# Attention and an FFT-mixed FFN on one core: batch 0's scores and values as two streams, index tables behind the first loads, and new durations in the planner

## The chip, the cores and the metric

The kernel runs on one core of one Trainium2 chip. The metric is the device time of one execution in microseconds (us). Five engines each work through an instruction queue of their own, in order: PE (matrix products), DVE, ACT and POOL (element work), and SP, which here only issues DMA transfers. Semaphores tie the queues together.

## The reference

q, k and v have 8 batches, 12 heads, 448 rows and 64 columns. All arithmetic of the reference is float32.

```python
scores = q @ k.transpose(0, 1, 3, 2) / sqrt(64)
attn   = maximum(scores, 0) ** 2 / 448
x      = (attn @ v) with the heads side by side     # (8, 448, 768)
u      = x + real(fft(fft(x, axis=1), axis=2))
un     = (u - mean(u)) / sqrt(var(u) + 1e-6)        # over the 768 columns
out    = u + maximum(un @ w_ch1, 0) @ w_ch2         # 768 -> 3072 -> 768
```

## The kernel before

**Stages.** Matrix products take bf16 operands. For each batch the heads are worked in pairs (m, 0 to 5). q and k are turned on PE for batches 0 and 1 (`turn_on_pe`, L505, copied out of PSUM at L510), later by DMA transposes (L469 copies, L481 transposes). A pair has four score chunks (c, 0 to 3). For each chunk there are two score products (L736), a Relu on ACT out of PSUM (`squares`, L761) and a square, mostly on DVE (`square`, L776, on ACT at L773). Four finished chunks feed eight value products (L718), which add up in one PSUM bank. `fold` then takes that bank out to bf16 in two halves (`leave`, L542 for batch 0, L557 or L554 later) and adds and subtracts its mirrored halves (L587, L589). The sums go through a DFT over the channels (`first_channels`, L1187, for batch 0; `mix`, L1212, later) and one over the rows (`rows` in `first_tail`, L823 and L827; `mix_rows`, L1026 and L1030, later), which gives u. Rows of u are normalised (un), turned (L926 for the first group of rows, L994 for the second), and go through the FFN: first layer L1452 with its Relu on DVE (L1424) or ACT (L1426), second layer L1477, L1503 and L1583, added to u at L1438.

**Tables.** `build_dft` makes cosine and sine tables. POOL writes index rows (`dft_indices`, L245 to L251), DVE turns them into phases (`turns`, L304 to L306), and ACT takes the sine (L310). The row tables (seqm, nseq) need two sets of 240 columns, the channel tables (chan, three of them) one set of 386 columns each. The pairs 3 to 5 need the channel table's second half with its sign changed, `chan_neg`, made by DVE (L333).

**The order of the work.** The body runs under a manual schedule. Each part is a generator that asks for an engine with `need(engine, duration, what must be ready, buffers)`; `Streams.run` keeps a planned clock for each engine and always emits the instruction that can start first by that clock (ties by rank). The durations (`mm`, `act`, `dve`, `dve2`, `SWITCH`, `LATENCY`) and the planned landing of loads thus decide the order in each queue, and nothing else. The emitted order is fixed; on the chip each queue waits at its own semaphores.

**Batch 0.** `attention(0)` is one stream: it emits the scores of one chunk at a time, and the eight value products of a pair together, after the scores of the same step. Where PE has nothing planned, `warming` emits filler products on zeros (L1661) until the DFT over the channels of batch 0 is done. `attentions` runs batches 1 to 7, interleaved with the FFN of earlier rows; `LEAD` limits how far it runs ahead.

**The first tail.** After batch 0's row DFT (four sets of rows, t from 0 to 3) `first_tail` is written out by hand: statistics on DVE (`stats` L847, `aggregate` L853), root on ACT (L859), `scale` on DVE (L867, L868), `norm` on POOL (L900) for the first three sets and on ACT (L902) and DVE (L905) for the last, `copy` of u (L876), `turn` on PE (L926, with filler products L924 and L931), `unload` out of PSUM (L941). The FFN starts when all four are unloaded.

**Loads.** POOL issues them in the order of `loading`: batch 0's three groups of q, k, v (L376), q and k of batch 1, the first weight in twelve pieces (L406), v of batch 1 among the second weight in four pieces (L416). SP issues the DMA transposes, the stores of u and the output.

Of the kernel before, what the change touches and what calls it, by code (L numbers as in the profile page):

```python
# [57 lines left out]


LATENCY = {"PE": 0.28, "ACT": 0.18, "DVE": 0.16, "POOL": 0.2, "SP": 0.1}  # L60


class Streams:
# [29 lines left out]
    def run(self):  # L93
        end = {}
        while self.streams:
# [61 lines left out]
def dve2(n):  # L157
    return Port(n / 1920 + 0.14)


SWITCH = 0.13


@with_exitstack
def kernel(
# [132 lines left out]
    def build_dft():  # L298
# [27 lines left out]
        for m in range(3):  # L326
            e = yield need("DVE", 1.5, [indices_ready])
            y = early_hid if m == 2 else work.tile([128, 4 * KH], FP32, name="dfty", tag=("u1A", "u1B")[m], bufs=1)
            turns(y[:, 2 * KH:4 * KH], y[:, 0:2 * KH], col2, row[:, 4 + m:5 + m], 2 * KH, m % 2)
            yield from sine(chan[m][:, 0, :], y[:, 0:2 * KH], 2 * KH, e, -1, halfpi)  # L330
            yield from sine(chan[m][:, 1, :], y[:, 2 * KH:4 * KH], 2 * KH, e)
            e = yield need("DVE", 0.3, [dft_ready])
            nc.vector.tensor_scalar(chan_neg[:, m], chan[m][:, :, KH:], -1.0, None, op0=ALU.mult)  # L333
            dft_ready.t = chan_ready[m].t = e + LATENCY["DVE"]

# [26 lines left out]
    def load_group(i, which=(0, 1, 2)):  # L362
# [3 lines left out]
        for x, (nm, src) in enumerate((("q", q), ("k", k), ("v", v))):  # L366
            if x not in which:
                continue
            if b == 0 and x < 2:
                e = yield need("POOL", 0.85)  # L370
                t = first_qk[x][:R, g]
            else:
                e = yield need("POOL", 0.85, bufs=[BQ[x] if x == 2 else BQ[x][home(i)]])
                t = work.tile([R, HG, 4 * Dh], BF16, name=f"{nm}n",
                              tag="vn" if x == 2 else f"{nm}n{home(i)}", bufs=3 if x == 2 else 1)
            nc.gpsimd.dma_start(out=t, in_=src[b, hs].rearrange("h (p j) d -> p h (j d)", j=4))  # L376
            loads[i][x] = t.rearrange("p h (j d) -> p j h d", j=4)
# [12 lines left out]
            if i == NG + 1 and x == 1:  # L390
                yield need("POOL", 3.6)
                mirrors()
# [28 lines left out]
    def loading():  # L421
# [101 lines left out]
    def fold(b, m, F, av, give, av_end):  # L523
# [4 lines left out]
        def leave():  # L528
# [4 lines left out]
            else:  # L533
# [125 lines left out]
    def attention(b, left=None):  # L659
# [9 lines left out]
        while pa < NB:  # L669
# [38 lines left out]
            for part in ("scores", "values") if few else ("values", "scores"):  # L708
# [19 lines left out]
                for i in range(p, p + n):  # L728
                    m, c = divmod(i, 4)
                    qT, kT, flat = turned[b][m // 2]  # L730
                    wide = R if b < 2 else 128
                    k0 = (2 * c + m % 2) * R
                    sc = BS.take()
                    for h in range(2):
                        ps = slice(h * Dh, (h + 1) * Dh)
                        nc.tensor.matmul(sc[:wide, h, 0:S].rearrange("k (c q) -> k c q", c=4),  # L736
                                         lhsT=flat[ps, k0:k0 + wide], rhs=qT[ps, m % 2],
                                         start=True, stop=True)
# [4 lines left out]
                    if b == 0 and i == NB - 1:  # L743
                        first_scores.t = e
            p += n
# [4 lines left out]
            if av_end is not None:  # L750
                left = None
                yield from fold(bv, mv, Fv, av, give, av_end)

    def squares(b, scs, sqs):
        for i, sc, t in scs:
            e = yield need("ACT", act(2 * S) - 0.03, [t + LATENCY["PE"]], [BSQ])
            at = min(sq_ids)
# [41 lines left out]
    def first_tail(pcs):  # L799
# [88 lines left out]
        def norm(t, hf, en):  # L888
# [3 lines left out]
            if en == "POOL":  # L892
                deps.append(u_done[ch][i])
            d = {"ACT": act(D // 2), "DVE": dve(D // 2), "POOL": 2.0}[en]
            e = yield need(en, d, deps, [BUN[ch]] if i == 0 and hf == 0 else [])
# [11 lines left out]
            t_un[t][hf] = e + LATENCY[en]  # L907
            if min(t_un[t]) or en == "POOL":
                half_un[ch][i].t = max(t_un[t])
# [24 lines left out]

        def unload(t, en):
            n, idn, c0, w = turned_cols(t)
            g = groups[0][2]
            src = pts[t][0][:, :, 0:384].rearrange("p h (m w) -> p h m w", w=128)[:, :, :, 0:w]
            dst = g[:, :, c0:c0 + w].rearrange("p (h m) w -> p h m w", h=2)
            last = yield need(en, (act if en == "ACT" else dve)(6 * w), [done[t][0]])  # L940
            (nc.scalar.copy if en == "ACT" else nc.vector.tensor_copy)(dst, src)  # L941
            BS.give(pts[t][0], last)
            first_un[t].t = last + LATENCY["ACT"]
# [6 lines left out]
        for t in range(3):  # L950
# [35 lines left out]

    second_un = [Cell() for _ in range(5)]

# [394 lines left out]
    def ffn(b):  # L1383
# [83 lines left out]
        for c in WHOLES[b]:  # L1467
# [3 lines left out]
            for hf in range(2):  # L1471
# [192 lines left out]

    LEAD, MIXED, SPARE, ELASTIC = 2.6, 1, 0.5, (1, 99)
    with tc.manual_schedule():
# [7 lines left out]
        sch.add(mixes(), (1, 1))  # L1674
        sch.add(attention(0), (0, 0))
        for i in range(2):
# [40 lines left out]
```

## Time and profile before

| | |
|---|---|
| median of 3 runs | 584.73 us (584.64 to 585.35) |
| the profiled execution | 584.67 us, its span 582.8 us |
| mean granted PE clock | 0.997 |
| PE filler products L1661 | 204, from 1.3 to 39.4 us |
| first row product of batch 0 (L823) | 40.64 us |
| first FFN product (L1452) | 53.63 us |
| last FFN product (L1583) | starts at 578.97 us |

Times in the profile are us from the first instruction. In the lists of instructions the columns are start, length, engine, line, operation, tiles written and read, shapes and count; what stands in brackets is how long the engine was idle before it and who released it. A row of several merged instructions has the length from the first one's start to the last one's end. Consecutive instructions of one engine overlap a little, so start to start is the better price. In a table of windows each engine has its busy time and its instructions (x).

### The profile page before, as it was taken

The page shows a single profiled execution, that of the slowest core. Times are in us where ns is not written, and L with a number is a line of the kernel's source. Part 1 is how long each engine was busy: PE and PEld are TensorE (multiplying, and loading weights), DVE is VectorE, ACT ScalarE, POOL GpSimd, SP SyncE. Part 2 cuts the span into 40 slices and gives each one's busy share as a digit, 9 for nine tenths or more (in the row PEclk, how much of TensorE's full clock was granted, in tenths as well). Part 3 has the DMA queues.
Part 4 walks back from the last instruction along what each step waited for, and adds up shares of the span by engine and source line. Part 5 has one row for each costly group of instructions (what it writes and reads, how often), then busy time and mean ns, then how long its engine had stood idle before and what let it go on. Part 6 is the DMA issues. An engine that isn't in the chain of part 4 may idle for free.

```text
span 582.8 us, 11457 instructions
## 1 busy us (share of the span) xinstructions
PE 572.9 (98%) x4476; PEld 365.7 (63%) x4476; DVE 406.4 (70%) x927; ACT 335.0 (57%) x511; POOL 133.7 (23%) x188
## 2 busy tenths in 40 slices
PE   8999999999999999999999999999999999999997
PEld 7566556544455546556857667568577786868684
DVE  5978667986669988787787878987946852222222
ACT  5866873587745787676668748777654340304040
POOL 8534021411115313421333032303300230000000
PEclk9998999999999999999999999999999999999999
DMA  9999999776947997699579987993433353031201
GB/s 120 206 211 227 222 210 134 173 131 95 181 57 189 207 172 168 116 216 167 122 123 207 180 153 147 200 176 115 126 75 100 118 151 99 30 94 36 79 30 55
DMA packets 133493, 81.85 MB, mean 140 GB/s; under 512 B 77504, under 2 KB 128704, under 8 KB 133440
## 3 DMA queue, kind: packets, MB, share of 16 engines
q0 software_dynamic: 40320, 33.63, 38.2%
q1 hardware_dynamic: 93120, 47.50, 36.3%
q8 instruction: 35, 0.57, 0.4%
q14 instruction: 18, 0.15, 0.1%
HBM read 62.91 MB, written 26.25 MB: 153 GB/s over the span
## 4 chain that ended last, share of the span: by engine, by line
PE 88%; DVE 6%; ACT 4%; issue 1%; POOL 0%; DVEq 0%; ACTq 0%; POOLq 0%
PE psF L1452 37%; PE psF L1583 26%; PE psS L736 6%; PE psF L718 5%; PE psF L1503 3%; PE psF L1477 3%; PE psS L1212 2%; ACT sq L761 2%; DVE sq L776 2%; PE psS L718 1%; PE psS L823 1%; PE psS L1026 1%; PE psS L1187 1%; PE psF L505 0%; ACT un L1087 0%
## 5 line engine op out<-in xcount | busy, mean ns | idle before, releaser
L1452 PE MATMUL psF<-unT,w 128*128 128x256 bf16 (+2 forms) x1728 | 229.8, 291 | 1.2 <-ACT unT L999 0.9
L1452 PEld LDWEIGHTS <-w 128*128 128x128 bf16 x1728 | 165.9, 98 | 61.6 <-issue 11.5
L761 ACT ACTIVATE sq<-psS 112x896 bf16<-112x896 f32 x192 | 164.4, 918 | 38.4 <-PE psS L736 38.0
L1426 ACT ACTIVATE hT<-psF 128x512 bf16<-128x512 f32 (+3 forms) x169 | 87.9, 532 | 116.6 <-PE psF L1452 115.8
L776 DVE TENSOR_TENSOR sq<-sq 112x896 bf16<-112x896 bf16 x161 | 100.6, 638 | 16.6 <-ACT sq L761 15.6
L1583 PEld LDWEIGHTS <-hT 128*128 128x128 bf16 x792 | 76.0, 98 | 54.4 <-issue 5.8
L1438 DVE TENSOR_TENSOR o<-psF,o 128x384 f32<-128x384 f32 x92 | 50.9, 553 | 44.8 <-PE psF L1583 39.6
L1583 PE MATMUL psF<-w,hT 128*128 128x384 bf16 x462 | 81.7, 326 | 0.3 <-DVE hT L1424 0.2
L736 PE MATMUL psS<-qkT 64*128 64x448 bf16 (+1 forms) x384 | 51.6, 359 | 1.2 <-ACT qkT L510 0.4
L718 PE MATMUL psF<-sq,vn 112*64 112x448 bf16 x320 | 37.9, 358 | 0.3 <-DVE o L1438 0.3
L557 DVE TENSOR_SCALAR xT<-psF 128x224 bf16<-128x224 f32 x58 | 19.8, 383 | 26.3 <-PE psF L718 26.2
L376 POOL DMA_DIRECT2D vn<-in_v_dram x24 | 17.3, 720 | 76.0 <-PE psS L736 67.7
L1059 POOL TENSOR_TENSOR u<-tp,xn 112x385 f32<-112x385 f32 (+2 forms) x14 | 13.3, 953 | 93.1 <-DVE tp L1041 81.5
L1583 PE MATMUL psF<-wsum,hT 128*128 128x384 bf16 x198 | 34.6, 326 | 0.0
L736 PEld LDWEIGHTS <-qkT 64*128 64x128 bf16 (+1 forms) x384 | 15.9, 102 | 28.7 <-issue 21.2
L376 POOL DMA_DIRECT2D qn<-in_q_dram x21 | 15.5, 739 | 69.9 <-DVE qkr L469 49.6
L718 PEld LDWEIGHTS <-vn 112*64 112x64 bf16 x384 | 17.8, 109 | 21.4 <-issue 13.7
L773 ACT ACTIVATE sq<-sq 112x896 bf16<-112x896 bf16 x31 | 29.5, 956 | 0.5
L1068 DVE BATCH_NORM_STATS2 stats<-u 112x6 f32<-112x384 f32 (+2 forms) x56 | 28.4, 541 | 0.0
L1087 ACT ACTIVATE un<-u,nmr,rstd 112x768 bf16<-112x768 f32 (+2 forms) x22 | 22.4, 1025 | 7.3 <-DVE nmr L1074 5.0
L1477 PE MATMUL psF<-w,hT 128*128 128x384 bf16 x144 | 25.1, 326 | 0.0
L1503 PE MATMUL psF<-w,hT 128*128 128x384 bf16 x144 | 24.7, 326 | 0.0
(166 smaller groups left out, 612.6 us busy)
## 6 DMA issues: line engine op xcount, KB each, us to landing
out_dram<-o SPq DMA_DIRECT2D x56, 192.0 KB, 2.2
vn<-in_v_dram POOLq DMA_DIRECT2D x24, 224.0 KB, 5.9
qn<-in_q_dram POOLq DMA_DIRECT2D x21, 224.0 KB, 5.3
kn<-in_k_dram POOLq DMA_DIRECT2D x21, 224.0 KB, 5.5
w<-in_moe_w_ch_dram POOLq DMA_DIRECT2D x12, 384.0 KB, 14.5
w<-in_moe_w_ch_dram POOLq DMA_DIRECT2D x4, 1152.0 KB, 20.5
utop<-u SPq DMA_DIRECT2D x12, 336.0 KB, 3.1
o<-utop SPq DMA_DIRECT2D x16, 192.0 KB, 3.8
```

The source lines that it names most:

```text
L376: nc.gpsimd.dma_start(out=t, in_=src[b, hs].rearrange("h (p j) d -> p h (j d)", j=4))
L718: nc.tensor.matmul(av[h * Dh:(h + 1) * Dh, 0:S], lhsT=vn[:, c, h0 + h, :], rhs=sq[:, h, :], start=(c == 0), stop=(c == 3))
L736: nc.tensor.matmul(sc[:wide, h, 0:S].rearrange("k (c q) -> k c q", c=4), lhsT=flat[ps, k0:k0 + wide], rhs=qT[ps, m % 2], start=True, stop= ...
L761: nc.scalar.activation(r, sc[:R, :, 0:S], AF.Relu)
L773: nc.scalar.activation(r, r, AF.Square)
L776: nc.vector.tensor_tensor(r, r, r, op=ALU.mult)
L1426: nc.scalar.activation(hs, ps, AF.Relu)
L1438: nc.vector.tensor_tensor(o, pc[:, 0:DH], o, op=ALU.add)
L1452: nc.tensor.matmul(ph[:, i * N:(i + 1) * N], lhsT=w1_sb[m][hf][:, (jj + i) * 128:(jj + i + 1) * 128], rhs=unT[:, m, 0:N], start=(m == 0), ...
L1477: nc.tensor.matmul(pc[:, 0:DH], lhsT=block(j, c), rhs=w2(j, hf), start=(j == 0), stop=(j == JC - 1))
L1503: nc.tensor.matmul(pc[:, 0:DH], lhsT=block(2 * i + k, c), rhs=weights[i], start=(start and i == 0), stop=(i == KP - 1), skip_group_check=True)
L1583: nc.tensor.matmul(pc[:, 0:DH], lhsT=lhs[i], rhs=rhs[i], start=(start and i == 0), stop=(i == KP - 1), skip_group_check=True)
```

## The change

- **Two streams for batch 0.** `first_attention` emits score chunks only; for each pair it adds a stream `first_values`, which asks for the two value products of each chunk as soon as that chunk is squared, instead of all eight together.
- **The planner's durations.** `mm`, `act` and `SWITCH` are shorter; an engine's planned clock advances by less than the duration on ACT and DVE (`OVERLAP`); loads of batches 2 and later are planned to land earlier (2.0 and 1.0 instead of 14.0 and 7.0 us of allowance); `LEAD` is 2.8 instead of 2.6. This changes the order on all engines through the whole program.
- **Tables.** The index rows come right after the first q and k loads, ahead of the identity matrix and the first v load. `chan_neg` is made on POOL (`negative`).
- **The last exit of batch 0.** For pair 5 one half of the exit is on ACT, the other on DVE.
- **First tail.** Statistics and aggregate of the last set come ahead of the third set's norm; the last unload is split, one half on ACT and one on DVE, and goes ahead of the last copies of u.
- **Weights.** Three of the four loads of the second weight wait in POOL's queue behind the third norm (`first_norms`). `w2_free` is set by the last whole block alone.

```diff
+OVERLAP = {"ACT": 0.12, "DVE": 0.07}
-            self.engine[eng] = start + dur
+            self.engine[eng] = start + max(dur - OVERLAP.get(eng, 0.0), 0.5 * dur)
 def mm(n):
-    return n / 2400 + 0.006
+    return n / 2400 + 0.002
 def act(n):
-    return n / 1200 + 0.2
+    return n / 1200 + 0.17
-SWITCH = 0.13
+SWITCH = 0.1
...
-            e = yield need("DVE", 0.3, [dft_ready])
-            nc.vector.tensor_scalar(chan_neg[:, m], chan[m][:, :, KH:], -1.0, None, op0=ALU.mult)
-            dft_ready.t = chan_ready[m].t = e + LATENCY["DVE"]
+            sch.add(negative(m, dft_ready.t), (0, 0))
+
+    def negative(m, t):
+        e = yield need("POOL", 0.4, [t])
+        nc.gpsimd.tensor_scalar(chan_neg[:, m], chan[m][:, :, KH:], -1.0, None, op0=ALU.mult)
+        dft_ready.t = chan_ready[m].t = e + LATENCY["POOL"]
...
-            ready[i][x].t = sch.dma(e, GRP, 360e3, "sw") + (1.5 if g else 0.0, 3.0, 14.0, 7.0)[min(b, 3)]
+            ready[i][x].t = sch.dma(e, GRP, 360e3, "sw") + (1.5 if g else 0.0, 3.0, 2.0, 1.0)[min(b, 3)]
             if i == 0 and x == 1:
-                yield need("POOL", 0.7)
-                make_identity(nc, ident)
-            if i == 0 and x == 2:
                 e = yield need("POOL", 1.1)
                 dft_indices()
                 indices_ready.t = e + LATENCY["POOL"]
+                yield need("POOL", 0.7)
+                make_identity(nc, ident)
...
         yield from load_group(NG + 2, (2,))
+        yield need("POOL", 0.0, [first_norms])
         yield from load_w2([1, 2, 3])
...
-            if b == 0:
+            if b == 0 and m == MC - 1:
+                t1 = yield need("ACT", act(HS), [av_end], [BX[m]])
+                nc.scalar.activation(xa[0], xa[1], AF.Copy, scale=1.0 / (64.0 * S))
+                t = yield need("DVE", dve(HS), [av_end])
+                nc.vector.tensor_scalar(xb[0], xb[1], 1.0 / (64.0 * S), None, op0=ALU.mult)
+                t = yield need("DVE", 2 * dve2(NS), [t1 + LATENCY["ACT"]])
+            elif b == 0:
...
+    def first_attention():
+        F, sqs = [], {}
+        for i in range(4 * MC):
+            m, c = divmod(i, 4)
+            e = yield need("PE", mm(S) + 2 * SWITCH, [turned_at[0][m // 2][m % 2]], [BS])
+            sc = score(0, i)
+            if i == 4 * MC - 1:
+                first_scores.t = e
+            sqs[i] = [None, Cell(), None]
+            sch.add(squares(0, [(i, sc, e - SWITCH)], sqs), (0.2, 0.2))
+            if c == 3:
+                if m % 2 == 1:
+                    BQT.free.append(e)
+                sch.add(first_values(m, F, sqs), (0.1, 0.1))
+
+    def first_values(m, F, sqs):
+        vn, h0 = loads[m // 2][2], 2 * m % HG
+        for c0, c1 in ((0,1),(1,2),(2,3),(3,4)):
+            e = yield need("PE", (c1 - c0) * mm(S) + 2 * SWITCH,
+                           [sqs[4 * m + c][1] for c in range(c0, c1)] + [ready[m // 2][2]],
+                           [BF] if c0 == 0 else [])
+            if c0 == 0:
+                av = BF.take()
+            for c in range(c0, c1):
+                sq, _, at = sqs.pop(4 * m + c)
+                sq_ids.append((e, at))
+                BSQ.free.append(e)
+                for h in range(2):
+                    nc.tensor.matmul(av[h * Dh:(h + 1) * Dh, 0:S], lhsT=vn[:, c, h0 + h, :], rhs=sq[:, h, :],
+                                     start=(c == 0), stop=(c == 3))
+        if m % 2 == 1:
+            BQ[2].free.append(e)
+        yield from fold(0, m, F, av, lambda when: BF.give(av, when), e - SWITCH + LATENCY["PE"])
...
-        def unload(t, en):
+        def unload(t, en, part=None):
...
+            hs = slice(0, 2) if part is None else slice(part, part + 1)
+            src = pts[t][0][:, hs, 0:384].rearrange("p h (m w) -> p h m w", w=128)[:, :, :, 0:w]
+            dst = g[:, :, c0:c0 + w].rearrange("p (h m) w -> p h m w", h=2)[:, hs]
...
         yield from stats(3, 0)
+        yield from stats(3, 1)
+        yield from aggregate(3)
         yield from scale(2)
         yield from norm(2, 0, "POOL")
-        yield from stats(3, 1)
-        yield from aggregate(3)
         yield from turn(0, 0)
         yield from root(3)
...
         yield from unload(2, "ACT")
+        yield from turn(3, 0)
+        yield from unload(3, "ACT", 0)
+        yield from unload(3, "DVE", 1)
         yield from copy(3, 0, "ACT")
-        yield from turn(3, 0)
-        yield from unload(3, "DVE")
         yield from copy(3, 1, "DVE")
...
-            w2_free.t = e + LATENCY["PE"]
+            if c == WHOLES[b][-1]:
+                w2_free.t = e + LATENCY["PE"]
...
-    LEAD, MIXED, SPARE, ELASTIC = 2.6, 1, 0.5, (1, 99)
+    LEAD, MIXED, SPARE, ELASTIC = 2.8, 1, 0.5, (1, 99)
...
-        sch.add(attention(0), (0, 0))
+        sch.add(first_attention(), (0, 0))
```

More of the change, by code (lines that the diff above doesn't have):

```diff
@@ L729, in attention @@
                     m, c = divmod(i, 4)
[L730 to L738, printed above, removed]
+                    sc = score(b, i)
                     scs.append((i, sc, e - SWITCH - (4 * mm(S) + SWITCH if values and few else 0.0)
@@ L752, in attention, with score @@
                 yield from fold(bv, mv, Fv, av, give, av_end)
+    def first_attention():
[15 more added lines that the diff above has]
+        for c0, c1 in ((0,1),(1,2),(2,3),(3,4)):
+            e = yield need("PE", (c1 - c0) * mm(S) + 2 * SWITCH, [sqs[4 * m + c][1] for c in range(c0, c1)] + [ready[m // 2][2]],
+                           [BF] if c0 == 0 else [])
[11 more added lines that the diff above has]
+        yield from fold(0, m, F, av, lambda when: BF.give(av, when), e - SWITCH + LATENCY["PE"])
+    def score(b, i):
+        m, c = divmod(i, 4)
+        qT, kT, flat = turned[b][m // 2]
+        wide = R if b < 2 else 128
+        k0 = (2 * c + m % 2) * R
+        sc = BS.take()
+        for h in range(2):
+            ps = slice(h * Dh, (h + 1) * Dh)
+            nc.tensor.matmul(sc[:wide, h, 0:S].rearrange("k (c q) -> k c q", c=4), lhsT=flat[ps, k0:k0 + wide],
+                             rhs=qT[ps, m % 2], start=True, stop=True)
+        return sc
     def squares(b, scs, sqs):
         for i, sc, t in scs:
-            e = yield need("ACT", act(2 * S) - 0.03, [t + LATENCY["PE"]], [BSQ])
+            e = yield need("ACT", act(2 * S), [t + LATENCY["PE"]], [BSQ])
             at = min(sq_ids)
@@ L893, in norm @@
                 deps.append(u_done[ch][i])
-            d = {"ACT": act(D // 2), "DVE": dve(D // 2), "POOL": 2.0}[en]
+            d = {"ACT": act(D // 2), "DVE": dve(D // 2), "POOL": 1.0}[en]
             e = yield need(en, d, deps, [BUN[ch]] if i == 0 and hf == 0 else [])
@@ L933, in turn @@
                 yield need("PE", 16 * 0.055)
-        def unload(t, en):
+        def unload(t, en, part=None):
             n, idn, c0, w = turned_cols(t)
             g = groups[0][2]
-            src = pts[t][0][:, :, 0:384].rearrange("p h (m w) -> p h m w", w=128)[:, :, :, 0:w]
-            dst = g[:, :, c0:c0 + w].rearrange("p (h m) w -> p h m w", h=2)
-            last = yield need(en, (act if en == "ACT" else dve)(6 * w), [done[t][0]])
+            hs = slice(0, 2) if part is None else slice(part, part + 1)
+            src = pts[t][0][:, hs, 0:384].rearrange("p h (m w) -> p h m w", w=128)[:, :, :, 0:w]
+            dst = g[:, :, c0:c0 + w].rearrange("p (h m) w -> p h m w", h=2)[:, hs]
+            last = yield need(en, (act if en == "ACT" else dve)((6 if part is None else 3) * w), [done[t][0]])
             (nc.scalar.copy if en == "ACT" else nc.vector.tensor_copy)(dst, src)
+            t_un[t][part or 0] = last
+            if part == 0:
+                return
+            if part == 1:
+                last = max(t_un[t])
             BS.give(pts[t][0], last)
@@ L984, in first_tail @@
         sch.add(turn_rows(uns[0][1], max(t_un[1]), 128, rev[:, 63:127], 0, 64, "DVE", second_un[0]), (1, 1))
-    second_un = [Cell() for _ in range(5)]
+    second_un, first_norms = [Cell() for _ in range(5)], Cell()
     def turn_rows(un, t, n, idn, c0, w, en, done):
```

4 lines of the change are left out of this document (2 added, 2 removed).

## The prediction

> **What bounds the kernel now.** I read the page first (busy shares, slices), then the DVE timeline of the opening, the windows by stage, the waits, and the ACT timeline around 120 us.
>
> ```profile
> PE 572.9 (98%) x4476; PEld 365.7 (63%) x4476; DVE 406.4 (70%) x927; ACT 335.0 (57%) x511; POOL 133.7 (23%) x188
> ```
>
> PE looks full, but 204 of its matmuls are fillers (L1661) that do no work, all before 39.4 us. The windows show the stages:
>
> ```profile
> core 0: us, PE busy (x) PEld busy (x) DVE busy (x) ACT busy (x) POOL busy (x), PEclk, DMA share, GB/s
> 7.93:39.52 31.59, 30.42 (x385) 19.32 (x385) 28.43 (x66) 26.30 (x35) 15.29 (x46) 1.00 1.18 197
> 40.64:52.74 12.10, 10.75 (x112) 7.96 (x112) 8.90 (x26) 7.96 (x18) 9.05 (x11) 1.00 1.24 222
> 60.00:460.00 400.00, 397.82 (x2920) 238.11 (x2917) 317.18 (x718) 261.63 (x398) 96.92 (x110) 1.00 0.85 152
> ```
>
> From 60 us on PE stands still for only 2.2 us of 400, so the end moves only by what the opening (batch 0's attention, 7.93 to 39.52), the first tail (40.64 to 52.74) and the few PE gaps later give. In the opening the busiest worker that does real work is DVE, 28.43 of 31.59 us, with its waits in view:
>
> ```profile
> 7.93 0.62 DVE L510 COPY qkT<-psF 128x896 bf16<-128x896 bf16 x1 [0.32 <-PE psF L505]
> ...
> 11.18 0.63 DVE L776 TENSOR_TENSOR sq<-sq 112x896 bf16<-112x896 bf16 x1 [0.18 <-ACT sq L761]
> ...
> 13.81 0.27 DVE L333 TENSOR_SCALAR channeg<-chan 128x386 bf16<-128x386 bf16 x1 [0.38 <-ACT chan L310]
> ...
> 38.26 0.69 DVE L542 TENSOR_SCALAR xT<-psF 128x224 bf16<-128x224 f32 x2 [0.96 <-PE psF L718]
> ```
>
> DVE waits for ACT while four squares are ready one by one, then for the sine, and at the end 0.96 us for the last values, which stood on PE behind 16 transposes and 14 matmuls of L1187.
>
> **The sum is made** against the profiled execution: 584.67 us, its span 582.8 and 1.87 around it. The median of the runs is 584.73, so I add the change to the median. About 0.2%, 1.2 us, is what a measurement of this kernel can tell from no change.
>
> **Opening, DVE's work.** Both kernels start at the same DVE copy (7.93): it waits for the first loads, whose issues do not move. By starts (overlaps of consecutive instructions taken off):
> - One set of table steps L304, L305, L306 moves ahead of that copy: 13.99 to 15.57 is 1.58 us. It fits there: the index iotas now follow the k load (its issue ends at 2.96) instead of the v load (4.21), 1.25 earlier, so the first tables end at 7.62 - 1.25 = 6.37 and the set at 7.95.
> - The three sign copies L333 go to POOL: 13.81 to 13.99, 3 x 0.18 = 0.54.
> - One half of the last exit L542 goes to ACT: 0.30 (17.70 to 18.00).
>
> Together 2.42 us less. **DVE's waits**, by starts: before, 0.31 for the first square, 0.27 for each of three more (0.80 apart, while a square takes 0.53 back to back: 2.67 for five), 0.47 for L333, 0.7 for four later squares, 1.04 for the last exit: 3.3. After: ACT now does both sines of table 0 and the copy L510 ahead of the squares. Sines start at 6.40; three at 0.59, two at 0.51, the copy 0.80: first square at 10.0, done at 10.9; DVE is free at about 10.05, so 0.85; then 0.27, and 0.78 where a sine (0.51) stands between. From there on ACT needs 24 x 0.80 + 4 x 0.51, done by 31.3 and always ahead of DVE. At the end three quarters of the last values are already on PE, since each quarter follows its square; what is left is 0.5. Sum 2.4, so 0.9 less. Opening: -3.3.
>
> The halved exit is not parallel: in the built program the DVE half carries a wait for the ACT half, which the change writes first. So 0.36 and 0.30 in a row stand in place of 0.68; nothing is gained there beyond DVE's 0.30. The same with the last unload of the tail.
>
> **What the POOL copies cost.** A POOL tensor operation on 768 columns takes 0.98 (L900), so 386 take about 0.49. Next to such work DVE is held:
>
> ```profile
> 405.58 1.27 DVE L776 TENSOR_TENSOR sq<-sq 112x896 bf16<-112x896 bf16 x1 [0.29 <-ACT sq L761]
> ```
> ```profile
> 405.40 0.98 POOL L1084 TENSOR_SCALAR un<-u,rstd,nmr 113x768 bf16<-113x768 f32 x1 [5.49 <-DVE nmr L1074]
> ```
>
> The square took 1.27 instead of 0.62 and began its work, it seems, when POOL ended. The first of the three copies falls into DVE's 0.85 us wait, the other two among squares: between 0 and 3 x 0.49 = 1.5 on DVE; I take 0.6, nearer the row shown, as one copy is covered and POOL may also be the one that waits. [...]
>
> **POOL's queue.** Everything behind the copies waits for a sine. Batch 0's third v load slips from 8.63 to 9.9 and is first used after 26; the w1 loads slip from 17.16 to about 20.2, while the last load ahead of them lands at 22.2, so their queue does not run dry and w1 ends near 45.6, before its first use near 50. The first v load is issued 0.9 later (8.2 to 9.1 at landing, used near 12). Three w2 loads go behind the third norm L900, near 47 to 49; with the page's 20.5 us from issue to landing, and some more as they queue behind each other, they are there by 70 to 76, and first needed near 88 (L1477 began at 91.7). All at nothing; without that cover each us late would be a us.
>
> **First tail.** Rows take PE 6.9 us in both. Before, from 40.64: third POOL norm at +8.4, last norm on ACT at +10.1, last turn on PE at +10.85, last unload ended +12.1. After: one more statistics step (0.56) and an aggregate (0.21) come before the third norm, which slips by 0.8; the last norm, no longer behind the late root, ends 0.3 earlier, at +10.5. PE turns it by +11.0, ACT unloads the third turn by +11.2, then its half of the last (about 0.45, from 0.77 for the whole on DVE), then DVE its half (0.4): +12.1 again. Nothing; bounds -0.4 and +0.8.
>
> **Later.** The planner's new durations change the order everywhere, not the work: the matmul counts are equal but for 102 fillers less. The largest PE wait after 60 us:
>
> ```profile
> PE psF L1452 <- ACT unT L999: 0.9, 1, 0.9
> ```
> ```profile
> 120.28 1.93 ACT L1087 ACTIVATE un<-u,nmr,rstd 112x768 bf16<-112x768 f32 x2
> 122.12 2.51 ACT L761 ACTIVATE sq<-psS 112x896 bf16<-112x896 f32 x3
> 124.51 0.66 ACT L999 CAST unT<-psS 128x582 bf16<-128x582 f32 x1
> ```
>
> Three L761 stand between the norms and the unload that PE needs. In the changed order none does, and matmuls of L1477 follow the last turn, so 0.9 and about 0.3 of gaps around it go: -1.2. Bounds -2.2 (all gaps after 60 us) and +1.5 (as much again elsewhere).
>
> **Clock.**
>
> ```profile
> 12.94:16.36 3.42, 2.90 (x53) 1.00 1.46 195
> ...
> 50.49:53.90 3.41, 2.08 (x35) 1.00 1.13 252
> 53.90:57.32 3.42, 3.42 (x26) 0.50 1.26 208
> ```
>
> The columns after the length: PE busy, clock granted, DMA share, GB/s. After a stretch with PE busy 2.08 of 3.41 us the clock is halved for 3.41 us; 2.90 did not do that. Price: at most half the stretch, 1.7; six matmuls of L1452 took 1.88 there against 1.14 elsewhere, so I put 1.1. The tail keeps its gaps, so the price stays: 0, bounds -1.1 and +1.7. In the opening the fillers fall by 102 x 0.055 = 5.6 us: (30.42 - 5.6) over 28.9 (31.59 less 2.7) is 0.86, or 2.93 of 3.41, a mean hardly over 2.90; single stretches may lie lower. [...]
>
> Sum: -3.3 + 0.6 + 0 - 1.2 + 0 = -3.9; 584.73 - 3.9 = 580.8.
>
> **Rivals.**
> - *The clock falls in the opening* (ends slower). Place: stretches of 9.5 to 33 us, where fillers are gone. Half a stretch, 1.7, each; a halved stretch counts as busy, so every other one: four, +6.8, 587.6. It decides from three on (5.1 = 3.9 + 1.2). For: 2.08 was enough once. Against: 2.90 was not, PE has slack there, so the price is an upper end. 0.06.
> - *The later order gives nothing or costs*: the DVE copies L469, which wait for transposes, stop the queue elsewhere, and PE pays 1.5: 580.8 + 1.2 + 1.5 = 583.5, worse if PE pays more. For: those waits were 4.2 us in four. Against: PE paid for none. 0.14, a third of it within 0.2%, a fifth slower.
> - *POOL holds DVE each time*: +0.9, 581.7. For: 1.27. 0.10.
> - *The clock stays whole after the tail*, since more scores and transposes follow it: -1.1, 579.7. 0.12.
> - *The opening is the planner's wish only*: PE queues quarters of values ahead of squares that are late, DVE's waits stay 3.3 and POOL costs 1.5: 580.8 + 0.9 + 0.9 = 582.6. 0.10.
>
> **Numbers.** Forecast itself 0.48, at 580.8. Faster by over 0.2% (below 583.6): 0.86; within: 0.05; slower: 0.09 (the first rival, and the second's end). Range: bounds of opening and later terms rarely fall together; 578.5 (whole clock, all gaps gone) to 583.4 leaves out under 2 in 10.
>
> **What would show it.** DVE's last L589 ends near 36.8 instead of 39.52; the first L823 near 38.0; DVE's exit half starts after ACT's; tail length 12.1; no PE wait on L999; 0.50 clock once only. Wrong if the fold ends later than 38.5, if stretches before 35 us show a clock under 1.00, or if PE busy in the 400 us after the opening falls under 396.

## The result, and the profile after

The changed kernel takes 588.61 us (median of 6 runs, 587.9 to 590.76) against 584.68 for the kernel before on the same chip: ratio 1.0074, 95% interval 1.0054 to 1.0093. It is slower by about 4 us; forecast were 580.8 and a range to 583.4. The profiled execution took 588.44 us (span 586.7), 3.77 more than that of before. The ratios here and below leave out runs in the chip's slower state, and need not be the quotients of the medians.

First the page's row of busy shares, then the same windows as before; the second one starts here at 38.91, where the first row product (now L872) lies.

```profile
PE 569.1 (97%) x4369; PEld 360.9 (62%) x4374; DVE 415.9 (71%) x937; ACT 327.2 (56%) x500; POOL 139.1 (24%) x190
```
```profile
core 0: us, PE busy (x) PEld busy (x) DVE busy (x) ACT busy (x) POOL busy (x), PEclk, DMA share, GB/s
7.93:39.52 31.59, 27.24 (x273) 15.25 (x271) 27.71 (x63) 27.08 (x38) 20.58 (x50) 1.00 1.10 175
38.91:51.84 12.93, 10.89 (x112) 8.04 (x112) 8.40 (x26) 8.10 (x19) 8.69 (x10) 1.00 1.15 227
60.00:460.00 400.00, 393.84 (x2886) 235.53 (x2888) 329.14 (x738) 251.79 (x384) 97.79 (x109) 1.00 0.85 155
```

The opening did get shorter: the first row product is 1.73 us earlier (38.91, was 40.64). The tail became longer: its last unload ends 12.93 us after that product (12.09 before). The loss is in the 400 us behind: PE stands still for 6.16 us of them, before for 2.18. From the first row product to the last FFN product it is 543.90 us against 538.33; -1.73 + 5.57 makes the 3.84 by which the last product starts later (582.81, was 578.97).

The waits of PE, with the releaser, us in total, times, longest:

```profile
PE psF L729 <- DVE o L1496: 1.7, 2, 1.2
PE psF L1510 <- DVE xT L568: 1.7, 2, 1.3
PE psS L977 <- POOL un L949: 1.4, 2, 0.8
...
PE psF L1642 <- DVE xT L568: 1.1, 1, 1.1
```

The 0.9 us for the unload behind three Relus (L999 in the kernel before) is gone. In its place PE waits for DVE: at 154 (L1510), 186 and 310 (L729) and 302 (L1642), 1.32, 1.24, 0.49 and 1.06 us, together 4.1. What DVE did just before 186 and 302, and POOL beside it:

```profile
181.62 2.78 DVE L825 TENSOR_TENSOR sq<-sq 112x896 bf16<-112x896 bf16 x1 [0.30 <-issue]
...
300.04 2.64 DVE L1119 TENSOR_TENSOR u<-tp,xn 112x383 f32<-112x383 f32 x1
```
```profile
181.06 1.10 POOL L1180 DMA_INDIRECT nbot<-un,backe  x1 [5.90 <-ACT un L1145]
182.19 0.92 POOL L1117 TENSOR_TENSOR u<-tp,xn 112x385 f32<-112x385 f32 x1
183.06 0.85 POOL L1119 TENSOR_TENSOR u<-qs,xn 112x383 f32<-112x383 f32 x1
```

A square that elsewhere takes 0.62 us takes 2.78: it ends 0.49 us after POOL's second add (183.91), so, by its end, it did its work when POOL was done. The add at 300 is the same case; the exit for which PE waits (L568) comes right behind it in DVE's queue. In both, two POOL adds in a row lie beside the long operation. Not every DVE operation beside them is long: at 352.14 an add with one input in PSUM (o, L1496) took its usual 0.55 us beside POOL's first add (352.10), and the square right behind it (352.61) took 1.71.

The wait at 154 is another one. DVE's copy of k (L474) waits 2.88 us for an earlier DMA transpose, which SP issued at 148.65, behind nine reads of rows of u into o (L1428):

```profile
154.79 0.43 DVE L474 COPY qkr<-kn 112x1024 bf16<-112x1024 bf16 x1 [2.88 <-DMA qkT<-qkr]
```
```profile
141.73 2.15 SPq L486 DMA_TRANSPOSE qkT<-qkr  x1
143.93 0.59 SPq L1428 DMA_DIRECT2D o<-ubot  x1
...
148.65 1.30 SPq L486 DMA_TRANSPOSE qkT<-qkr  x1
```

### The profile page after: what moved, and what is told of

Same layout as the page of the kernel before. It is cut to its first block, busy times and chain, and to the rows that moved or that the text cites. A ratio compares the mean times of both kernels' runs of the same rounds, so it can differ in the third digit from the quotient of the medians.

```text
span 586.7 us, 11266 instructions
## 1 busy us (share of the span) xinstructions
PE 569.1 (97%) x4369; PEld 360.9 (62%) x4374; DVE 415.9 (71%) x937; ACT 327.2 (56%) x500; POOL 139.1 (24%) x190
## 4 chain that ended last, share of the span: by engine, by line
PE 74%; DVE 10%; DMA 6%; ACT 5%; POOL 2%; issue 2%; SPq 1%; POOLq 0%; DVEq 0%; ACTq 0%
PE psF L1510 31%; PE psF L1642 24%; PE psS L799 5%; PE psF L729 4%; PE psF L1562 3%; ACT sq L810 2%; DMA xn<-xT 2%; DMA qkT<-qkr 2%; PE psS L1270 2%; DVE sq L825 2%; DMA w<-in_moe_w_ch_dram 2%; PE psF L1535 1%; DVE stats L1126 1%; PE psS L729 1%; DVE u L1119 1%
## 5 line engine op out<-in xcount | busy, mean ns | idle before, releaser
L1510 PE MATMUL psF<-unT,w 128*128 128x256 bf16 (+2 forms) x1723 | 230.5, 290 | 2.9 <-DVE xT L568 1.7
L1510 PEld LDWEIGHTS <-w 128*128 128x128 bf16 x1728 | 165.4, 98 | 65.4 <-issue 13.9
L1484 ACT ACTIVATE hT<-psF 128x512 bf16<-128x512 f32 (+3 forms) x162 | 84.5, 535 | 124.6 <-PE psF L1510 124.3
L825 DVE TENSOR_TENSOR sq<-sq 112x896 bf16<-112x896 bf16 x166 | 104.1, 643 | 15.0 <-ACT sq L810 14.1
L1642 PEld LDWEIGHTS <-hT 128*128 128x128 bf16 x792 | 76.0, 98 | 55.3 <-issue 5.4
L1642 PE MATMUL psF<-w,hT 128*128 128x384 bf16 x462 | 81.3, 326 | 0.0
L1496 DVE TENSOR_TENSOR o<-psF,o 128x384 f32<-128x384 f32 x92 | 50.6, 550 | 42.4 <-PE psF L1642 39.2
L1642 PE MATMUL psF<-wsum,hT 128*128 128x384 bf16 x198 | 34.8, 326 | 1.1 <-DVE xT L568 1.1
L729 PE MATMUL psF<-sq,vn 112*64 112x448 bf16 x280 | 33.2, 358 | 1.8 <-DVE o L1496 1.7
L568 DVE TENSOR_SCALAR xT<-psF 128x224 bf16<-128x224 f32 x60 | 20.5, 383 | 19.4 <-PE psF L729 19.4
L1117 POOL TENSOR_TENSOR u<-tp,xn 112x385 f32<-112x385 f32 (+2 forms) x14 | 13.1, 934 | 72.5 <-DVE tp L1099 69.0
L1145 ACT ACTIVATE un<-u,nmr,rstd 113x768 bf16<-113x768 f32 (+2 forms) x23 | 22.9, 1023 | 11.7 <-DVE nmr L1132 11.7
L1624 DVE TENSOR_TENSOR s<-hT 128x768 bf16<-128x768 bf16 x11 | 6.1, 551 | 31.8 <-ACT hT L1484 31.8
L729 PEld LDWEIGHTS <-vn 112*64 112x64 bf16 x336 | 16.0, 109 | 20.5 <-issue 13.5
L822 ACT ACTIVATE sq<-sq 112x896 bf16<-112x896 bf16 x26 | 24.8, 959 | 0.4
L1535 PE MATMUL psF<-w,hT 128*128 128x384 bf16 x144 | 24.9, 326 | 0.0
```

The costliest lines, as they stand in the source:

```text
L729: nc.tensor.matmul(av[h * Dh:(h + 1) * Dh, 0:S], lhsT=vn[:, c, h0 + h, :], rhs=sq[:, h, :], start=(c == 0), stop=(c == 3))
L822: nc.scalar.activation(r, r, AF.Square)
L825: nc.vector.tensor_tensor(r, r, r, op=ALU.mult)
L1484: nc.scalar.activation(hs, ps, AF.Relu)
L1496: nc.vector.tensor_tensor(o, pc[:, 0:DH], o, op=ALU.add)
L1510: nc.tensor.matmul(ph[:, i * N:(i + 1) * N], lhsT=w1_sb[m][hf][:, (jj + i) * 128:(jj + i + 1) * 128], rhs=unT[:, m, 0:N], start=(m == 0), ...
```

## The experiments

Theory: the loss is the new order after the tail, in which DVE is held by POOL where PE needs DVE. Rivals: the new opening hands loads and buffers over badly; or the new durations as such do no harm and the new streams do.

"PE idle" is 400 us less PE's busy time from 60 to 460 us. "Row" is the start of the first row product, "tail" the time from there to the end of the last unload; both from the one profiled execution. Medians are over all runs; the ratios are against the kernel before on the same chip, and carry the verdicts. Before's own medians there were 584.2 to 585.0, with single runs from 582.9 to 591.6. A profiled execution need not be a typical one: graft's (582.59 us) is the fastest of its runs, those of reverse (589.59), reverse_no_add (586.18) and graft_loads (589.13) are the slowest of theirs.

| kernel | median us | ratio to before, 95% interval | row | tail | PE idle |
|---|---|---|---|---|---|
| before | 584.7 | | 40.64 | 12.09 | 2.18 |
| changed | 588.61 | 1.0074 (1.0054 to 1.0093) | 38.91 | 12.93 | 6.16 |
| old_plan | 587.62 | 1.0061 (1.0035 to 1.0087) | 40.60 | 11.96 | 4.26 |
| new_plan | 595.10 | 1.0180 (1.0153 to 1.0206) | 42.67 | 12.10 | 11.15 |
| no_pool_add | 586.83 | 1.0034 (1.0014 to 1.0055) | 42.59 | 11.93 | 3.19 |
| pair_turns | 589.12 | 1.0081 (1.0064 to 1.0098) | 38.92 | 12.89 | 7.91 |
| graft | 584.56 | 1.0004 (0.9982 to 1.0027) | 38.89 | 13.08 | 2.37 |
| graft_fill | 586.64 | 1.0047 (1.0023 to 1.0072) | 38.88 | 13.10 | 4.52 |
| graft_tail | 584.70 | 0.9996 (0.9972 to 1.0019) | 38.88 | 13.11 | 3.06 |
| graft_tables | 588.09 | 1.0063 (1.0032 to 1.0093) | 41.68 | 12.28 | 4.14 |
| graft_loads | 586.19 | 1.0020 (1.0002 to 1.0038) | 41.39 | 11.96 | 5.34 |
| graft_signs | 586.86 | 1.0018 (0.9983 to 1.0053) | 40.35 | 11.95 | 6.03 |
| graft_both | 585.86 | 1.0024 (1.0004 to 1.0043) | 40.32 | 11.94 | 4.87 |
| reverse | 587.84 | 1.0048 (1.0027 to 1.0069) | 40.62 | 11.79 | 7.07 |
| reverse_no_add | 584.11 | 0.9997 (0.9982 to 1.0013) | 40.65 | 12.06 | 4.09 |
| before_no_add | 585.42 | 1.0019 (1.0002 to 1.0036) | 40.66 | 11.79 | 4.20 |
| best | 591.67 | 1.0104 (1.0073 to 1.0136) | 38.88 | 11.96 | 5.99 |

**Durations or structure.** old_plan is the changed kernel with the planner's durations of before, new_plan the kernel before with the new ones:

```diff
-OVERLAP = {"ACT": 0.12, "DVE": 0.07}
+OVERLAP = {}
-    return n / 2400 + 0.002
+    return n / 2400 + 0.006
...
```

> The changed kernel with the planner's durations of before (mm, act, SWITCH, OVERLAP, LEAD, load allowances, the third norm's planned time, w2_free), everything else as changed. Theory 1, the later order costs: the changed opening and tail are worth -1.7 and +0.8 us to the end of the tail (first row product 38.91 against 40.64, tail 12.94 against 12.10), and the new durations +4.8 in PE gaps after 56 us. Then this kernel is at about 583.8 (582.5 to 584.7), with PE gaps after 56 us near the 3.3 of before. Theory 2, the new structure (weights behind the third norm, buffers of batch 0, sign copies on POOL) is what delays the later stages: about 588. Third possibility: any new order of the same quality scatters by some us, and the gaps come at other places: 585 to 588 with gaps of 4 to 7 us.

> The kernel before with the planner's new durations alone. Theory 1, the later order costs: 584.7 + 4.8 = about 589 (587 to 590), with gaps after 56 us of 6 us or more. Theory 2, the new structure costs: about 585, gaps near 3.3 us.

Neither theory as stated: each of the two alone is slower than before, and new_plan by far more than the 4 us expected. The time of old_plan is that of the third possibility named for it, a new order that scatters by some us. Any edit to durations or streams makes the planner lay out another order of the whole program. Four such orders have PE idle for 2.18, 4.26, 6.16 and 11.15 us.

**The order alone.** The planner was made to follow a list (SEQUENCE: the order in which the planner of the other kernel took its streams' steps) after the first tail. In graft the changed kernel's opening and tail are followed by the order of before on all five engines; reverse is the other way round.

```diff
+                        if s[3] == "/mixes,/first_tail,":
+                            self.left = ["/loading,"] + SEQUENCE
...
+            if self.left:
+                byname = {s[3]: s for s in self.streams}
+                for k, name in enumerate(self.left[:40]):
+                    s = byname.get(name)
...
+                    best, spare = ((False, max(t), 0), s), None
```

> The changed kernel up to the end of the first tail; from there on the instructions of every engine stand in the order of the kernel before, written out as a list that the planner follows. Theory 1, the loss is in the later order alone: the first row product comes 1.73 us earlier, the tail is 0.84 us longer, the rest is as before: 584.7 - 0.9 = about 583.8 (583.0 to 584.5), PE gaps after 56 us near the 20.5 us of before (the changed kernel has 26.0, counted from 0.05 us). Theory 2, the new opening hands over loads, buffers or weights later and the later stages pay for it whatever their order: 586 or more, gaps of 24 us or more. Where the clock is halved in the opening, as in the profile without POOL adds, the first row product comes at 42.6 instead of 38.9 and the time is up to 3.6 us longer.

> The kernel before up to the end of its first tail; from there on the instructions stand in the order of the changed kernel. Theory, the later order alone costs, and it costs by DVE being held while POOL adds and by one late DMA transpose: about 584.9 + 4 = 589 (587.5 to 590), with PE gaps above 1 us near 154, 186 and 302 (shifted by what the opening shifts). Rival, the later order only fits badly to the new opening's loads and buffers: 585 to 586, without these gaps.

Graft is at 1.0004, against 1.0074 for the changed kernel: the new order after the tail costs 4.1 us (0.0070 of 584.7). Reverse is at 1.0048 behind the old opening, with the same waits at the same places (1.20 at 154, 1.23 at 186, 1.05 at 303). So the new order costs 2.8 us behind the old opening too; why it costs more behind the new one is not shown. The gain of 0.9 expected of graft is not seen in its ratio, though the interval covers it.

**DVE held by POOL.** POOL's two adds for a set of u rows become memsets, which read nothing; the sum into these rows is left out. The order stays, on all engines.

```diff
-            eng.tensor_tensor(u[:n, 0:KN], ts[i][:n, 0:KN], x[:n, 0:KN], op=ALU.add)
+            if i:
+                eng.memset(u[:n, 0:KN], 0.0)
+            else:
+                eng.tensor_tensor(u[:n, 0:KN], ts[i][:n, 0:KN], x[:n, 0:KN], op=ALU.add)
...
```

> The changed kernel in the same order on all five engines; the two adds that POOL makes for each set of u rows are replaced by two memsets of the same tiles (the sum into these rows is left out). Theory A, DVE operations with two SBUF inputs are held while POOL reads SBUF: the square of 2.78 us at 181.6 and the add of 2.64 us at 300.0 fall to about 0.6 each, the PE gaps of 1.40 (186.1) and 1.22 us (302.0) go, total 2.6 less: about 586.0 (585.5 to 586.8). Theory B, these long operations have another cause (a late input, the DMA traffic): both stay over 2 us and the time stays at 588.6.

> The same with POOL's adds of the u rows replaced by memsets (these sums are left out). Theory, DVE held by POOL is most of what the order costs: 3 to 4 us less than with the adds, 585 to 586.5; the gap of about 1.5 near 154, which a DMA transpose makes, stays. Rival, the order costs by other waits: less than 1.5 us less.

> The kernel before with the same replacement, in its own order. Theory, the order of before meets the same holding (squares of 1.14, 2.58 and 1.27 us at 306, 360 and 406) where PE does not wait for it: 0 to 0.6 us less than before, 584.4 to 585. Rival, leaving the adds out is a gain in any order (less work on POOL, rows ready earlier): 3 us less, about 582, and then the comparison in the changed order says nothing on the order.

The same square in reverse and, where POOL only writes, in reverse_no_add:

```profile
181.75 2.77 DVE L1574 TENSOR_TENSOR sq<-sq 112x896 bf16<-112x896 bf16 x1 [0.30 <-ACT sq L1556]
```
```profile
180.97 0.62 DVE L1574 TENSOR_TENSOR sq<-sq 112x896 bf16<-112x896 bf16 x1
```

With the adds gone, PE's waits at 186, 303 and 310 are gone in both kernels, and reverse falls from 1.0048 to 0.9997, by 3.0 us. The control in the order of before does not fall: 1.0019. So the adds are dear only in the order in which they meet DVE operations that PE waits for. In reverse that is the whole loss. The changed kernel falls by 2.3 us of its 4.3, to 1.0034 in no_pool_add, in whose profile the clock was halved in the opening (below), so that its row came at 42.59.

In both long cases DVE's operation started while POOL still issued an indirect store (L1180), ahead of the adds. The store alone does not hold it: the square of 0.62 us in reverse_no_add lies beside the same store.

```profile
180.28 1.16 POOL L1926 DMA_INDIRECT nbot<-un,backe  x1 [8.92 <-ACT un L1891]
```

Why the long square was held some 0.6 us ahead of the first add's start is not shown.

**The late transpose.** In pair_turns SP issues both transposes of a pair in a row; the other engines keep their order.

```diff
+                    if x == 0:
+                        nc.sync.dma_start_transpose(out=both[:, 1], in_=qk[0])
+                        nc.sync.dma_start_transpose(out=both[:, 0], in_=qk[1])
```

> The changed kernel in the same order on PE, DVE, ACT and POOL; on SP the second DMA transpose of each q and k pair is issued right behind the first instead of up to nine o loads later (148.65 instead of about 143.9 in one place). Theory: the DVE copy that waited 2.88 us for that transpose at 151.8 no longer does, and the PE gap of 1.49 us at 154.2 goes: about 587.1 (586.6 to 587.6). If the gap has another cause (DVE full, DMA engines full), the time stays at 588.6.

The wait at 154 is gone, but a new one of 2.23 us stands at 106 (PE for DVE's L1103), and the time is no better: 1.0081. Ahead of it DVE stands 4.48 us for another transpose, where the changed kernel waits 0.64:

```profile
103.46 0.56 DVE L1121 TENSOR_TENSOR u<-tp,xn 128x383 f32<-128x383 f32 x1 [4.48 <-DMA xn<-xT]
```

The cause of the gap was right; with the remedy DVE waited for a transpose at another place.

**The opening, edit by edit**, on the grafted order, so that what follows the tail stays put:

```diff
 graft_tables:
+                yield need("POOL", 0.7)
+                make_identity(nc, ident)
+            if i == 0 and x == 2:
                 e = yield need("POOL", 1.1)
                 dft_indices()
 graft_signs:
-            sch.add(negative(m, dft_ready.t), (0, 0))
+            e = yield need("DVE", 0.3, [dft_ready])
+            nc.vector.tensor_scalar(chan_neg[:, m], chan[m][:, :, KH:], -1.0, None, op0=ALU.mult)
```

> The kernel with the grafted order, and the identity and the index rows in POOL's queue as in the kernel before (index rows behind the first v load). Theory as predicted: one set of table steps (1.58 us of DVE) goes back among the squares, the first qkT copy starts at 7.9 instead of 8.7; net 0.8 later, first row product near 39.7, time 0.8 over the grafted kernel. Rival, the set ahead of the copy was worth nothing, since it ran beside POOL's index rows at 2.5 times its length: first row product within 0.3 of the grafted kernel's.

> The kernel with the grafted order, and the three sign copies back on DVE (three operations of 0.18 us) instead of on POOL. Theory as predicted: no gain in the opening from moving them (0.54 us less on DVE, 0.6 us of holding), but POOL's queue no longer waits for the sines, so the first weight is issued some 2 to 3 us earlier, the loads in front of the first norm wait less, and the tail falls from 13.08 to about 12.1 us: 583.7. Rival, the copies on POOL were a real gain: first row product 0.5 us later, at 39.4, tail unchanged, 585.0.

Both moves were worth more than priced. Without the early tables the row comes 2.8 us later (expected 0.8), without the sign copies on POOL 1.46 later (expected: nothing). Each edit also rearranges the opening's order, so these are the values of the edits with that.

**The tail.** graft_tail has the tail's code of before; graft_loads puts two more loads of POOL's queue behind the third norm:

```diff
-        yield from load_w2([0])
-        yield from load_group(NG + 2, (2,))
         yield need("POOL", 0.0, [first_norms])
-        yield from load_w2([1, 2, 3])
+        yield from load_group(NG + 2, (2,))
+        yield from load_w2([0, 1, 2, 3])
```

> The kernel with the grafted order, and the first tail written as in the kernel before: third norm ahead of the last set's second statistics and aggregate, the last unload whole on DVE and behind one copy of u. Theory, the new order of the tail made it longer (12.94 against 12.10 us from the first row product to the last unload): about 0.8 us less than the grafted kernel, tail 12.1. Rival, the tail is as long because PE now has other work between its turns, or its POOL norms run beside other DVE work: tail 12.7 or more, same time.

> The kernel with the grafted order; in POOL's queue alone, two more loads (the last v of batch 1 and the first piece of the second weight) go behind the third norm. Theory, POOL came late to the norms because each of its loads waits for the load eight places ahead (the first norm started at 45.32, its inputs were there at 43.53): the first norm starts at 43.6, the three DVE operations of 1.28, 1.09 and 0.97 us beside the norms move but stay long, the tail falls from 13.08 to 12.1 us (11.4 to 12.4) and the time by 0.7 to 1.7 us, to about 583.4. Rival, the tail is set by the DVE operations that POOL's norms hold, wherever the norms lie: tail 12.8 or more, time as the grafted kernel's 584.6.

> Both edits, sign copies on DVE and two loads behind the third norm. If each works through POOL's late norms alone, they don't add: tail about 12.0 us, 583.4 to 583.8. If the first norm is still late after either of them, the two add: tail 11.5 us, 583.0.

Writing the tail as before changes nothing (13.11 against 13.08). What lengthened it shows in POOL's timeline of the changed kernel:

```profile
42.90 0.84 POOL L420 DMA_DIRECT2D w<-in_moe_w_ch_dram  x1 [1.15 <-DMA w<-in_moe_w_ch_dram]
44.83 0.72 POOL L381 DMA_DIRECT2D vn<-in_v_dram  x1 [1.09 <-DMA w<-in_moe_w_ch_dram]
45.59 1.95 POOL L949 TENSOR_SCALAR un<-u,rstd,nmr 128x768 bf16<-128x768 f32 x2
```

Each load waits until an earlier piece of the first weight has landed (in this trace the load eight places ahead in POOL's queue: the one at 44.83 for the piece issued at 29.98), and the first norm stands behind them. With the two loads behind the norms (best, whose opening is as early) it starts at 43.71 and waits for DVE alone:

```profile
43.71 0.98 POOL L1751 TENSOR_SCALAR un<-u,rstd,nmr 128x768 bf16<-128x768 f32 x1 [2.20 <-DVE nmr L1719]
```

The tail is then 11.96 us, 1.1 shorter than in graft_fill, which has the same opening and fillers and the loads in front (13.10). graft_loads and graft_both have this tail too, but their rows came later, so they alone don't show it; and in none of them did the time follow (1.0020 and 1.0024).

**Fillers, and all together.** graft_fill adds 42 fillers where PE waits in the opening. best has these, the two loads, and a store ahead of a q load at 192 us:

```diff
+            for _ in range((20, 0, 0, 6, 8, 8)[i] if i < 6 else 0):
+                nc.tensor.matmul(first_pps[0][:, 0, 2 * KH:512], lhsT=warm[:, 0:128], rhs=warm[:, 2 * KH:512],
+                                 start=False, stop=False)
```

> The kernel with the grafted order, and 42 more filler products on PE: 20 ahead of the first score, 22 ahead of scores 4 to 6, where PE waits. Theory, the clock in the opening hangs on where its windows fall: the 3.41 us stretch with the least work before 40 us rises from 1.4 to over 2.5 us of PE busy, no execution has the halved clock there, first row product at 38.9 to 39.2, and the median is 0 to 1.5 us under the grafted kernel's, by how many of its executions are halved. Rival, the fillers stand in the way of the scores: first row product and time 0.3 to 0.6 us later.

> The grafted order with three edits together: two loads behind the third norm, the 42 filler products where PE waits in the opening, and at 192 us one store of normalised rows ahead of a q load in POOL's queue. Theory: first row product at 38.9 in every execution (no halved clock before 40 us), first norm within 0.3 us of its inputs, tail 11.4 to 12.2 instead of 13.08, the PE gap near 205 (0 to 3.6 us in the runs with this order) down by about 1: 582.0 (581 to 583.3), under both kernels. Rival, the loads behind the norms or the fillers cost as much elsewhere, or the DMA chain of 205 stays: 584.5 or more.

The fillers delay nothing up to the tail (row 38.88, unload 51.98), yet graft_fill is at 1.0047; in its profile PE waits 1.90 us near 206 for a DMA transpose, where graft does not wait. best ends its tail at 50.84, 1.89 us ahead of before, and is the slowest of the grafts: 1.0104. Its profile (587.59 us) shows part of why: PE waits 1.90 us at 207 for a DMA transpose, and 1.12 at 390. Its median is 4 us above that profile, and what the other runs lost is not known. No version beat the kernel before.

## Why the prediction was wrong

**Later (-1.2, bounds -2.2 and +1.5): the step that failed.** From the last unload to the last product the changed kernel needs 530.97 us, before 526.24: +4.7. With -1.73 of the opening and +0.84 of the tail that is the whole 3.84 (-3.9 forecast), and PE's 393.84 us of work in the 400 is under the 396 that the prediction named as a sign of being wrong. The named gain came (no wait for the unload of L999). The upper bound, "as much again elsewhere", was taken from the gaps of the order that existed; it says nothing of an order not yet run. The mechanism was in the prediction, as the 1.27 us square beside POOL's norm, but it was priced for the three sign copies only. The profile of before has it at POOL's adds too, dearer, at a place where PE did not wait:

```profile
360.10 2.58 DVE L776 TENSOR_TENSOR sq<-sq 112x896 bf16<-112x896 bf16 x1
```
```profile
360.48 0.92 POOL L1059 TENSOR_TENSOR u<-tp,xn 112x385 f32<-112x385 f32 x1
361.35 0.84 POOL L1061 TENSOR_TENSOR u<-qs,xn 112x383 f32<-112x383 f32 x1
```

In the changed kernel POOL's adds are L1117 and L1119, and the built order showed which squares and exits stood beside them.

**The second rival** (the later order costs, 583.5, "worse if PE pays more") had the sign, and its mechanism is the wait at 154. Its price of 1.5 is about that one wait (1.32, and 1.20 in reverse); the larger part was not in it. At 0.14 it had far too little weight.

**Opening (-3.3 + 0.6 = -2.7): right in kind, -1.73 measured.** The last fold ends at 37.52 (36.8 forecast). The term that was mis-sized is the start: the first copy was to begin at 7.93 and began at 8.70, and the first square at 11.58 (10.9 forecast). From that copy to the last fold it is 28.82 us against 31.59, or 2.77 less, which is the sum's 2.7, and the fifth rival (DVE's waits stay) did not happen. Another 0.28 was lost between the fold and the row.

```profile
3.26 0.96 DVE L315 TENSOR_SCALAR drow<-drow 128x2 f32<-128x2 f32 x1 [2.04 <-POOL drow L246]
...
8.70 0.62 DVE L515 COPY qkT<-psF 128x896 bf16<-128x896 bf16 x1
...
15.34 0.74 DVE L307 SCALAR_TENSOR_TENSOR early<-early 128x386 f32<-128x386 f32 x1
...
36.55 0.40 DVE L548 TENSOR_SCALAR xT<-psF 128x224 bf16<-128x224 f32 x1 [0.63 <-ACT xT L546]
```

The two small scalings ahead of the first set took 0.96 and 0.88 us (0.38 and 0.30 before). They ran beside POOL's index rows in both kernels, so why they were longer is not shown. The sign copies were cheaper on DVE than feared and dearer on POOL: table steps beside them took 0.74 instead of 0.56, while the copies themselves took 1.30 to 1.55 us (0.49 forecast):

```profile
10.04 1.32 POOL L338 TENSOR_SCALAR channeg<-chan 128x386 bf16<-128x386 bf16 x1 [1.31 <-ACT chan L311]
```

As said, the halves of the exit ran one after the other (0.63 of waiting for ACT).

**POOL's queue ("all at nothing") and the tail (0): +0.84.** The tail's own working is not what failed: in graft_tail the old code gives the same length. The step that failed is the queue: the w1 loads began at 22.1 (20.2 forecast), each landed about 1.85 us after the other, and POOL, which waits for them ahead of its next loads, came late to the first norm. The cover was worked out for the loads' users, not for the norms behind the loads in the same queue.

**Clock (0): right for this execution.** It is halved once, after the tail, as before. That is partly luck: the one halving of 3.41 us makes a mean clock of 0.997 in both, while eight of the seventeen profiles have 0.999 or 1.000, so theirs stayed whole after the tail, which is the fourth rival, and one of the eight is before_no_add (0.999), with the opening and the tail of before. It happened in graft's profile too (0.999), whose 582.59 us holds that gain.

**The first rival is real, as a matter of chance.** Six profiles have the changed opening without extra fillers. In two of them the clock was halved near 11.7 us and stayed so, no_pool_add first, then graft_loads:

```profile
8.09:11.50 3.41, 1.64 (x20) 1.08 (x20) 2.91 (x6) 3.41 (x7) 2.11 (x3) 1.00 1.38 179
11.50:25.15 13.65, 13.53 (x90) 6.15 (x89) 10.12 (x19) 10.59 (x15) 11.97 (x38) 0.50 1.06 135
```
```profile
8.46:11.88 3.42, 1.76 (x20) 1.09 (x18) 2.85 (x6) 3.42 (x6) 2.11 (x3) 1.00 1.33 177
11.88:22.11 10.23, 10.23 (x66) 4.59 (x64) 7.84 (x16) 7.86 (x12) 8.68 (x33) 0.50 1.20 159
```

The price was 3.7 and 2.5 us at the first row product (38.9 otherwise). In the others the stretch that held PE's wait of 1.24 us for the late copy fell elsewhere and had 1.90 us or more of work, as 7.58 to 10.99 of the changed kernel (counted back from its halving at 51.95, in 13 steps of that halving's length). By that count one order of the opening has these stretches from 7.58, 8.09 and 8.46 on in three profiles. The rival's working was off in one point: it had every other stretch halved, but three or four followed each other, though PE was busy in them for 10.23 us of 10.23 and 13.53 of 13.65.

## What to carry to other kernels

Where an order comes out of planned durations, a change of these durations is a new order: price it by what runs of several such orders show, not by the gaps of the present one, and look in the built order for places where DVE operations that POOL's adds made longer here (a square 2.78 us instead of 0.62, an add for u 2.64 instead of 0.55) stand beside such adds and PE is next. Freezing the order behind an edit lets that edit be measured alone. In a queue that both issues loads and computes, look at what the loads wait for, and at the compute behind them.

## What the runs showed of the hardware that was not expected

- The same order gives different DMA waits in different kernels' executions: where unT is read back, near 205 us, PE waited not at all in before and graft, and up to 3.4 us in kernels that share their order there. The longest, in graft_signs:

```profile
PE psF L2308 <- DMA unT<-nbot: 3.4, 1, 3.4
```

- The clock was halved after a stretch with PE busy 1.64 (no_pool_add) or 1.76 (graft_loads) of 3.41 us in the opening, and not after 1.90 (changed kernel), 1.97 (pair_turns) or 2.46 (graft) there; near the tail 1.96 (changed kernel) and 2.08 (before) were followed by it. PE's busy share alone does not give the limit, and none of these stretches ahead of a halving was idle.
- An earlier opening is not passed on: best finished its tail 1.89 us ahead of before and ended later. Part of that are waits on DMA.
